# Attention loads: four blocks of values, queries nearer to their use, shorter clears, three loads on ScalarE's queue

## The chip, the cores and the metric

The kernel runs on one core of a Trainium2 chip. The metric is the device time of one execution in microseconds, the median of several runs of the same program. The core has five engines with instruction queues of their own: TensorE (PE in the profile, its weight loads PEld), VectorE (DVE), ScalarE (ACT), GpSimd (POOL) and SyncE (SP). Here SP does nothing but issue transfers between the chip's memory and the core's SBUF; 16 DMA engines carry them out. ScalarE and GpSimd can issue transfers as well.

## The reference, cut to what matters

Three layers follow one another: attention with 8 heads over 4 sequences of 576 tokens (2304 tokens in all), a layer of 8 experts of which each token takes one, and a plain layer with a squared ReLU.

```python
rel = pos[:, None] - pos[None, :]
mask_plain = (rel >= 0) & (rel < 32)                              # heads 0 to 3
mask_dil = (rel >= 0) & (rel < 128) & (rel % 4 == 0)              # heads 4 to 7
attn = softmax(where(mask, q @ k.T / 8, -1e9));  x = attn @ v     # [2304, 512]

e_idx = argmax(x @ w_gate);  gate_w = softmax(x @ w_gate)[e_idx]
eom = sigmoid(x @ w_output_gate)[e_idx]
y[mask] = gate_w * eom * (relu(x[mask] @ w1[e]) @ w2[e])          # mask: e_idx == e

out = (relu(y @ w_in) ** 2) @ w_out
```

## The kernel before, in words

The 2304 tokens are 18 blocks of 128. The attention takes them one after another (the loop over `i` in `attention`); the experts then run over windows of a list of tokens per expert, and the last layer over strips of 768 tokens. The change lies in the attention, with a small part in the ordering of the experts and in the loop for tokens that fit in no window.

**One block of the attention.** `qk_mm` computes the scores of a block with 16 products (32 rows each in the trace), `qk_a` adds the masks on VectorE, `qk_b` takes the maximum on VectorE and subtracts it on GpSimd, `ex` takes the exponential on ScalarE, `tr` transposes the result with the unit matrix on TensorE and copies it out on ScalarE, `pv_mm` multiplies with the values, `pv_x` divides by the sum on VectorE and writes x, and `xt` transposes x for the router. TensorE gets all this in the order in which the loop is written: in iteration `i` it has `tr(i)`, the scores of block `i + 2`, `xt(i - 1)`, and `pv_mm(i)`. So an operand that lands late stops everything behind it on TensorE. Blocks 0 and 1 have their scores ahead of the loop, with warm-up products around them (`warm`).

**The buffers.** Queries lie in three buffers of a pair of blocks (`load_q`). Keys lie in a ring of five blocks (`kf`, `LAP`); after every fifth block `wrap` copies the last block's keys in front of the ring on ScalarE. The values lie in a ring of `VR` blocks (`vb`). Keys and values of two heads stand on alternating partitions with zeros between, so each place of the ring is cleared once by VectorE and GpSimd (`clear_k`, `clear_v`) before its first load.

**The transfers.** Nearly all are issued by SP, in the order in which the program is written. A load waits for the last reader of its buffer, and also for the transfer that was issued eight places earlier, since eight completion semaphores take turns. Where SP waits, all later loads wait with it. Once four blocks or three are done, their x is stored (`store`, five transfers each); the router groups them (`GROUPS`), and each token's entry goes to the list of its expert by an indirect transfer of GpSimd (`scatter`). The lists (`meta_d`, 8 lists of 2560 rows of 64 bytes) are cleared by one transfer (`clear`) at iteration 3. When the first 11 blocks are routed, the largest expert is chosen; SP reads its number and loads its first weights (`load_w`) and the first rows of its list (`meta_load`), at iterations 13 and 14.

**The ordering of the experts.** `order_steps` is a generator: some 50 small VectorE instructions, each set between larger ones of the expert stage (`run_small`). Its last ones compute what the loop over spilled tokens needs (`spilled`), a loop that runs as often as there are groups of tokens beyond all windows.

Of the kernel before, what the change touches and what calls it, by code (L numbers as in the profile page):

```python
# [36 lines left out]
E = 8  # L37
# [5 lines left out]

HALF = WIN[0] // 2
MS = NT + 256
MR = 16
YC = sum(WIN) + 192
NEG = -8.0e9
# [7 lines left out]

VN = 16 * (D + 1)
VL = -(-2 * VN // 128) * 128
VR = 6
KW = (LAP + 1) * 4 * P + 3 * P  # L60


# [9 lines left out]
def attention_experts_kernel(ctx: ExitStack, tc: tile.TileContext, qB, kB, vB, wE, wF, consts, late, rows, out):  # L72
# [30 lines left out]
    er_t = cpool.tile([1, E], I32, name="er_t")  # L103
    of_t = cpool.tile([1, E], I32, name="of_t")
    c0_t = cpool.tile([1, 1], I32, name="c0_t")
    spill = cpool.tile([1, 2, NSPILL], I32, name="spill")
    nspill = cpool.tile([1, 1], I32, name="nspill")
    mt = cpool.tile([P, E + 1, 4, 4], I32, name="mt")

# [4 lines left out]
    def raw_tile():  # L114
        return stg.tile([P, 1024], F32, tag="raw", name="raw", bufs=3)
# [116 lines left out]
    def order_steps(tp):  # L232

        v = nc.vector
        sq, sq2, sp = [1, E, E], [1, 2, E, E], [1, NSPILL, E]

        def row(shape, name, dt=F32):
            return tp.tile([1] + shape, dt, name=name)

        def two(name):  # L240
            return tp.tile([1, E, E], F32, tag="sq", name=name, bufs=2)

        def across(a):
            return a.unsqueeze(1).to_broadcast(sq)

        def down(a):
            return a.unsqueeze(2).to_broadcast(sq)

        cnt = cs[:, 1, :]
        key = row([E], "key")  # L250
        yield v.scalar_tensor_tensor(out=key, in0=cnt, scalar=float(E), in1=rev, op0=ALU.mult, op1=ALU.add)
        yield v.scalar_tensor_tensor(out=key, in0=star[0:1, :], scalar=float(2 ** 20), in1=key, op0=ALU.mult, op1=ALU.add)
        gt = two("gt")
        yield v.tensor_tensor(out=gt, in0=across(key), in1=down(key), op=ALU.is_gt)
        rk = row([E], "rkk")
        yield v.reduce_sum(out=rk, in_=gt, axis=AX.X)
        sel = two("sel")
        yield v.tensor_tensor(out=sel, in0=across(rk), in1=down(io8), op=ALU.is_equal)
        pm = tp.tile([1, NSPILL, E], F32, tag="big", name="pm")[:, 0:2 * E].rearrange("p (a r) e -> p a r e", a=2)
        yield v.tensor_tensor(out=pm, in0=sel.unsqueeze(1).to_broadcast(sq2), in1=cs.unsqueeze(2).to_broadcast(sq2), op=ALU.mult)  # L260
        sr = row([2, E], "sr")
        yield v.reduce_sum(out=sr, in_=pm, axis=AX.X)
        v.tensor_copy(er_t, sr[:, 0, :])
        yield "order"

        def before(a, o):
            om = two("om")
            yield v.tensor_tensor(out=om, in0=across(a), in1=lt, op=ALU.mult)
            yield v.reduce_sum(out=o, in_=om, axis=AX.X)

        nw = row([E], "nw")
        yield v.tensor_tensor(out=nw, in0=sr[:, 1, :], in1=win, op=ALU.min)
        of = row([E], "of")
        yield from before(nw, of)

        big = row([1], "big1")
        yield v.tensor_scalar(out=big, in0=of[:, E - 1:E], scalar1=float(NT - WIN[-1]), scalar2=None, op0=ALU.is_lt)
        yield v.tensor_tensor(out=sr[:, 0, :], in0=win, in1=nw, op=ALU.subtract)
        yield "late"
        yield v.scalar_tensor_tensor(out=nw, in0=sr[:, 0, :], scalar=big, in1=nw, op0=ALU.mult, op1=ALU.add)  # L280
        yield from before(nw, of)
        v.tensor_copy(of_t, of)

        ws = two("ws")
        yield v.tensor_tensor(out=ws, in0=down(rk), in1=across(io8), op=ALU.is_equal)
        yield v.tensor_tensor(out=ws, in0=ws, in1=across(win), op=ALU.mult)
        s0 = row([E], "s0")
        yield v.reduce_sum(out=s0, in_=ws, axis=AX.X)
        yield v.tensor_scalar(out=big, in0=big, scalar1=-1.0, scalar2=1.0, op0=ALU.mult, op1=ALU.add)
        yield v.tensor_scalar(out=s0, in0=s0, scalar1=big, scalar2=None, op0=ALU.mult)  # L290
        yield v.tensor_tensor(out=nw, in0=cnt, in1=s0, op=ALU.subtract)
        yield "offsets"
        ci = row([E], "ci", I32)
        yield v.tensor_scalar(out=ci, in0=nw, scalar1=0.0, scalar2=float(P - 1), op0=ALU.max, op1=ALU.add)
        yield v.tensor_scalar(out=ci, in0=ci, scalar1=7, scalar2=None, op0=ALU.logical_shift_right)
        nt = row([E], "nt")
        yield v.tensor_copy(nt, ci)
        pe = row([E], "pe")
        yield from before(nt, pe)
        yield v.tensor_tensor(out=nt, in0=pe, in1=nt, op=ALU.add)  # L300

        base = row([E], "base")
        yield v.scalar_tensor_tensor(out=base, in0=pe, scalar=-float(P), in1=s0, op0=ALU.mult, op1=ALU.add)
        yield v.tensor_tensor(out=base, in0=base, in1=ems, op=ALU.add)
        ge = tp.tile([1, NSPILL, E], F32, tag="big", name="ge")
        yield v.tensor_tensor(out=ge, in0=io32.unsqueeze(2).to_broadcast(sp), in1=nt.unsqueeze(1).to_broadcast(sp), op=ALU.is_ge)
        ei = row([NSPILL], "ei")
        yield v.reduce_sum(out=ei, in_=ge, axis=AX.X)
        yield v.tensor_scalar(out=ei, in0=ei, scalar1=float(E - 1), scalar2=None, op0=ALU.min)
        yield v.tensor_copy(spill[:, 0, :], ei)  # L310
        yield v.tensor_tensor(out=ge, in0=ei.unsqueeze(2).to_broadcast(sp), in1=io8.unsqueeze(1).to_broadcast(sp), op=ALU.is_equal)
        yield v.tensor_tensor(out=ge, in0=ge, in1=base.unsqueeze(1).to_broadcast(sp), op=ALU.mult)
        yield v.reduce_sum(out=ei, in_=ge, axis=AX.X)
        yield v.scalar_tensor_tensor(out=ei, in0=io32, scalar=float(P), in1=ei, op0=ALU.mult, op1=ALU.add)
        yield v.tensor_scalar(out=ei, in0=ei, scalar1=0.0, scalar2=float(E * MS - P), op0=ALU.max, op1=ALU.min)
        yield v.tensor_copy(spill[:, 1, :], ei)
        yield v.tensor_scalar(out=nt, in0=nt, scalar1=float(NSPILL), scalar2=None, op0=ALU.min)
        yield v.tensor_copy(nspill, nt[:, E - 1:E])
# [24 lines left out]
    def attention():  # L343
# [13 lines left out]
        def warm(n):  # L357

            ps = ps_1.tile([P, 4, P], F32, tag="xt", name="warm")
            for _ in range(n):  # L360
                nc.tensor.matmul(out=ps, lhsT=ones, rhs=ones.unsqueeze(1).to_broadcast([P, 4, P]), start=True, stop=True)

        def load_q(i, n):
            q = wk.tile([P, 2, 4, P], F32, tag="q", name="q", bufs=3)
            a = i % 2
            nc.sync.dma_start(out=q[:, 0:n].rearrange("p i a s -> p (i a s)"), in_=qB[i // 2, :, a:a + n].rearrange("p i s -> p (i s)"))
            for j in range(n):
                q_t[i + j] = q[:, j]

# [22 lines left out]
        def clear_v(j, h2, engine):  # L392
            engine.memset(vb[:, h2, j], 0.0)
# [6 lines left out]
        load_k(1, 1)  # L400
        nc.vector.memset(ones, 1.0)
        warm(8)
        nc.vector.memset(kz[:, :, 0, 0:2, 96:P], 0.0)
        nc.vector.memset(kz[:, :, 0, 2:4], 0.0)
        load_q(1, 1)
        nc.sync.dma_start(out=masks.rearrange("p a b m -> p (a b m)"), in_=consts[:, o:o + 512])
        clear_k(3, nc.vector, nc.gpsimd)
        load_k(2, 1)
        load_q(2, 2)
        nc.sync.dma_start(out=ident, in_=consts[:, 0:P])  # L410
        clear_v(0, 0, nc.vector)
        clear_v(0, 1, nc.gpsimd)
        load_v(0, 1)
# [8 lines left out]
            nc.sync.dma_start(out=late_sb, in_=late)  # L422
            nc.sync.dma_start(out=rowc, in_=rows)

        z = raw_tile().bitcast(I32)[:, 0:MS * E * MR // P // 4]

        def clear():
            nc.sync.dma_start(
                out=meta_d.rearrange("(p a n) c -> p a (n c)", p=P, a=4), in_=z.unsqueeze(1).to_broadcast([P, 4, MS * E * MR // P // 4])
            )  # L430

        group_of = {i: n for n, g in enumerate(GROUPS) for i in g}
        sm_t, p_t, pt_t, o_t, x_t, xT_t, lg_t = {}, {}, {}, {}, {}, {}, {}
# [253 lines left out]
        nc.gpsimd.memset(z.rearrange("p (n c) -> p n c", c=MR)[:, :, 2:3], OOB)  # L687
        nc.gpsimd.memset(idw, 0)
        ex(0)
        load_q(4, 2)  # L690
        load_v(2, 2)
        warm(7)
        ends = {g[-1] + 1: n for n, g in enumerate(GROUPS)}
# [14 lines left out]
        for i in range(NB):  # L708
# [12 lines left out]
                wrap()  # L721
                load_k(n + 2, min(3, NB - n - 2))

            if i % 2 == 0 and i + 6 < NB:
                load_q(i + 6, 2)
            if i == 0:
                load_consts()
            if i == 3:
# [35 lines left out]
                scale(0)  # L764
            if i == NB - 1:
                conv_w(0, 1)
            if i == 0:
                for j in range(4, VR):
                    clear_v(j, 0, nc.vector)
                    clear_v(j, 1, nc.gpsimd)  # L770
                load_v(4, 2)
            if i % 2 == 1 and i + VR - 1 < NB:
                load_v(i + VR - 1, 2)
            if i in STORES:
# [747 lines left out]
    def spilled():  # L1522
# [5 lines left out]
        with ExitStack() as st:  # L1528
            sp = st.enter_context(tc.tile_pool(name="sp", bufs=1))
            ps = st.enter_context(tc.tile_pool(name="sps", bufs=2, space=PSUM))  # L1530
            with tc.For_i(0, total) as i:
                ev = loaded(spill[:, 0, ds(i, 1)], mybir.EngineType.SP, E - 1, "cut to the experts")[0]
                rv = loaded(spill[:, 1, ds(i, 1)], mybir.EngineType.SP, E * MS - P, "cut to the rows")[0]
                m = sp.tile([P, 4], I32, name="m")
                nc.sync.dma_start(out=m, in_=meta_d[ds(rv, P), 0:4])
                x = sp.tile([P, DM], F32, name="sx")
# [147 lines left out]
```

## Time and profile before

| | us |
|---|---|
| median of 3 runs (lowest to highest) | 724.68 (722.94 to 727.16) |
| the profiled execution | 724.47 |
| its span, first to last instruction | 722.8 |

The profile has one execution. Its page says PE 694.7 us busy (96% of the span), DVE 486.4 (67%), ACT 326.5 (45%), POOL 114.5 (16%); the DMA engines moved 138.11 MB at a mean of 191 GB/s, and the granted clock of TensorE was 0.998 of full speed. Times in all rows count from the first instruction. A row of a timeline gives the start, the time taken, the engine, the line, the operation, what it writes and reads, how many instructions were merged into the row, and in brackets how long the engine had been idle and what ended that. SPq is the issuing of a transfer by SP, not the transfer. Since shares over the whole span mix stages, the stretch in which the changed code runs has to be read by itself.

### The profile page before, as it was taken

How to read it: one execution, taken by the hardware profiler on the slowest of the kernel's cores; microseconds unless marked ns; L12 is line 12 of the kernel's file. 1: busy time of each engine (PE TensorE's matmuls, PEld its weight loads, DVE VectorE, ACT ScalarE, POOL GpSimd, SP SyncE). 2: the span in 40 equal slices, each digit the busy share in tenths (PEclk: the TensorE clock that was granted, in tenths of full speed). 3: DMA queues.
4: the chain of work that ended last, by engine and by line, in shares of the span. 5: the costliest groups of instructions: out<-in, count | busy, mean ns of one | idle time of the engine just before them, and what ended most of it. 6: DMA issues, size and time to landing. Idle time of an engine off the chain costs nothing.

```text
span 722.8 us, 13818 instructions
## 1 busy us (share of the span) xinstructions
PE 694.7 (96%) x5203; PEld 631.9 (87%) x5203; DVE 486.4 (67%) x878; ACT 326.5 (45%) x599; POOL 114.5 (16%) x120
## 2 busy tenths in 40 slices
PE   7988889999999999989999999999999999999995
PEld 4766789999999999989999999999988888888884
DVE  7866775773646567668886878787889854445441
ACT  2443544543455555556555545565534422122120
POOL 6245336202010110008000000000000040012003
PEclk9999999999999999999999999999999999999999
DMA  8999556865475776862657545556755453235302
GB/s 281 414 338 316 183 165 210 261 182 162 157 221 158 229 239 190 245 203 64 219 165 249 194 152 195 193 203 231 238 170 196 139 177 108 91 119 162 110 22 91
DMA packets 65503, 138.11 MB, mean 191 GB/s; under 512 B 12838, under 2 KB 40023, under 8 KB 64407
## 3 DMA queue, kind: packets, MB, share of 16 engines
q1 hardware_dynamic: 53538, 121.60, 51.9%
q0 software_dynamic: 3984, 10.22, 4.1%
q10 hardware_dynamic: 7909, 5.35, 2.3%
q8 instruction: 43, 0.70, 0.4%
q14 instruction: 29, 0.24, 0.1%
HBM read 102.06 MB, written 35.12 MB: 190 GB/s over the span
## 4 chain that ended last, share of the span: by engine, by line
PE 68%; issue 10%; DVE 2%; DMA 2%; POOL 1%; ACT 1%; ACTq 0%; POOLq 0%; DVEq 0%; SPq 0%
PE op L1489 6%; PE op L1490 6%; PE op L1491 6%; PE bank_b L881 5%; PE bank_b L879 4%; PE bank_b L880 4%; PE yp L879 4%; PE yp L880 4%; PE hp L879 4%; PE yp L881 4%; PE hp L880 4%; PE hp L881 4%; PE bank_d L881 2%; PE bank_d L880 2%; PE bank_d L879 2%
## 5 line engine op out<-in xcount | busy, mean ns | idle before, releaser
L1454 DVE TENSOR_TENSOR slot_d<-gq,slot_d 128x768 fp32r<-128x768 f32 x48 | 45.9, 957 | 63.8 <-ACT slot_d L1452 62.3
L1452 ACT CAST slot_d<-gq 128x768 fp32r<-128x768 f32 x48 | 40.0, 835 | 95.2 <-PE op L1490 83.1
L1499 POOL DMA_INDIRECT out<-os,idc x18 | 20.0, 1112 | 352.9 <-DVE os L1498 348.3
L893 ACT ACTIVATE hh<-hp 128x240 fp32r<-128x240 f32 (+5 forms) x72 | 29.2, 410 | 42.3 <-PE hp L881 40.4
L1445 DVE SCALAR_TENSOR_TENSOR gq<-gq 128x768 f32<-128x768 f32 x48 | 45.7, 952 | 2.1 <-DMA gq<-g_d 2.1
L173 POOL DMA_INDIRECT xg<-x_d,mt x24 | 25.7, 1069 | 135.2 <-PE xp L197 123.2
L150 DVE TENSOR_TENSOR slot_d<-raw,slot_d 128x1024 fp32r<-128x1024 f32 x24 | 29.2, 1223 | 20.6 <-ACT slot_d L146 20.1
L1489 PE MATMUL op<-slot_b,slot_d 128*128 128x512 f32 x108 | 42.0, 389 | 0.0
L1490 PE MATMUL op<-slot_b,slot_d 128*128 128x512 f32 x108 | 42.0, 389 | 0.0
L1489 PE MATMUL op<-slot_a,slot_d 128*128 128x512 f32 x108 | 42.0, 389 | 0.0
L1490 PE MATMUL op<-slot_a,slot_d 128*128 128x512 f32 x108 | 42.0, 389 | 0.0
L1491 PE MATMUL op<-slot_a,slot_d 128*128 128x512 f32 x108 | 42.0, 389 | 0.0
L1491 PE MATMUL op<-slot_b,slot_d 128*128 128x512 f32 x108 | 42.0, 389 | 0.0
L894 DVE SCALAR_TENSOR_TENSOR hl<-hp,hh 128x240 fp32r<-128x240 f32 (+5 forms) x72 | 31.5, 449 | 14.8 <-ACT hh L893 12.1
L914 ACT COPY ys<-yp 128x240 f32<-128x240 f32 (+5 forms) x36 | 14.4, 399 | 48.8 <-PE yp L881 42.5
L880 PE MATMUL yp<-hl,slot_b 128*128 128x240 f32 (+3 forms) x112 | 31.8, 284 | 0.3 <-DVE hl L894 0.3
L879 PE MATMUL yp<-hh,slot_b 128*128 128x240 f32 (+3 forms) x112 | 32.1, 286 | 0.0
L150 DVE TENSOR_TENSOR slot_b<-raw,slot_b 128x1024 fp32r<-128x1024 f32 x20 | 24.2, 1220 | 11.4 <-ACT slot_b L146 11.0
L881 PE MATMUL yp<-hh,slot_b 128*128 128x240 f32 (+3 forms) x112 | 31.7, 283 | 0.0
L879 PE MATMUL hp<-xh,slot_d 128*128 128x432 f32 (+3 forms) x96 | 30.5, 318 | 0.3 <-DVE hl L894 0.3
L880 PE MATMUL hp<-xl,slot_d 128*128 128x432 f32 (+3 forms) x96 | 30.2, 315 | 0.0
L881 PE MATMUL hp<-xh,slot_d 128*128 128x432 f32 (+3 forms) x96 | 30.2, 314 | 0.0
(338 smaller groups left out, 2277.5 us busy)
## 6 DMA issues: line engine op xcount, KB each, us to landing
raw<-in_wE SPq DMA_DIRECT2D x64, 512.0 KB
g_d<-cr SPq DMA_DIRECT2D x96, 192.0 KB
gq<-g_d SPq DMA_DIRECT2D x48, 384.0 KB
raw<-in_wF SPq DMA_DIRECT2D x32, 512.0 KB
vb<-in_vB SPq DMA_DIRECT2D x16, 520.0 KB
yr<-yT_d SPq DMA_DIRECT2D x16, 384.0 KB
q<-in_qB SPq DMA_DIRECT2D x8, 512.0 KB
kf<-in_kB SPq DMA_DIRECT2D x8, 256.0 KB
```

Source lines behind the costliest of these rows:

```text
L150: nc.vector.tensor_tensor(out=lo, in0=raw_t.pop((r, c)), in1=hi.bitcast(F32), op=ALU.subtract)
L879: nc.tensor.matmul(out=out, lhsT=wh, rhs=mh, start=first, stop=False, skip_group_check=shared)
L880: nc.tensor.matmul(out=out, lhsT=wh, rhs=ml, start=False, stop=False, skip_group_check=shared)
L881: nc.tensor.matmul(out=out, lhsT=wl, rhs=mh, start=False, stop=last, skip_group_check=shared)
L893: nc.scalar.activation(out=h[:, :n], in_=p[:, :n], func=ACTF.Relu)
L894: nc.vector.scalar_tensor_tensor(out=l[:, :n], in0=p[:, :n], scalar=0.0, in1=h[:, :n].bitcast(F32), op0=ALU.max, op1=ALU.subtract)
L1445: nc.vector.scalar_tensor_tensor(out=x, in0=x, scalar=0.0, in1=x, op0=ALU.max, op1=ALU.mult)
L1452: nc.scalar.copy(out=h, in_=x)
L1454: return lambda: nc.vector.tensor_tensor(out=l, in0=x, in1=h.bitcast(F32), op=ALU.subtract)
L1489: nc.tensor.matmul(out=o_t[j], lhsT=h[:, a], rhs=w[:, 0], start=f == 0, stop=False)
L1490: nc.tensor.matmul(out=o_t[j], lhsT=h[:, a], rhs=w[:, 1], start=False, stop=False)
L1491: nc.tensor.matmul(out=o_t[j], lhsT=l[:, a], rhs=w[:, 0], start=False, stop=f == 15)
```

## The change

It has five parts:

1. `VR` falls from 6 to 4. The values of blocks 4 and 5 are no longer loaded into places of their own at iteration 0, whose four clears go; all pairs from block 4 on are loaded at odd iterations into places that have been read, `load_v(i + 3, 2)` instead of `load_v(i + 5, 2)`. The last pair is so issued at iteration 13, behind the first expert weights.
2. Queries: the load of blocks 4 and 5 ahead of the loop goes, and at even iterations `load_q(i + 4, 2)` takes the place of `load_q(i + 6, 2)`.
3. `clear` writes the first 512 rows of each list (`CLEARED`) instead of all 2560. The loop over spilled tokens writes the 128 rows behind a list's end itself; `order_steps` computes those ends (six VectorE instructions more).
4. The masks, the unit matrix and the queries of block 1 are issued by ScalarE instead of SP, behind a small exponential of the ones.
5. The first table load of ScalarE is now that of the small exponential; it is its first instruction in both kernels.

```diff
-VR = 6
+VR = 4
+CLEARED = -(-WIN[0] // 128) * 128
@@ order_steps
+        ends = row([E], "ends")
+        yield v.tensor_tensor(out=ends, in0=cnt, in1=ems, op=ALU.add)
...
+        yield v.tensor_tensor(out=ge, in0=ei.unsqueeze(2).to_broadcast(sp), in1=io8.unsqueeze(1).to_broadcast(sp), op=ALU.is_equal)
+        yield v.tensor_tensor(out=ge, in0=ge, in1=ends.unsqueeze(1).to_broadcast(sp), op=ALU.mult)
+        fi = row([NSPILL], "fi")
+        yield v.reduce_sum(out=fi, in_=ge, axis=AX.X)
+        yield v.tensor_copy(spill[:, 2, :], fi)
@@ attention, ahead of the loop
         warm(8)
+
+        nc.scalar.activation(out=wk.tile([P, 1], F32, tag="first", name="first", bufs=1), in_=ones[:, 0:1], func=ACTF.Exp)
+        nc.scalar.dma_start(out=masks.rearrange("p a b m -> p (a b m)"), in_=consts[:, o:o + 512])
+        nc.scalar.dma_start(out=ident, in_=consts[:, 0:P])
+        load_q(1, 1, nc.scalar)
...
-        load_q(1, 1)
-        nc.sync.dma_start(out=masks.rearrange("p a b m -> p (a b m)"), in_=consts[:, o:o + 512])
...
-        nc.sync.dma_start(out=ident, in_=consts[:, 0:P])
...
-        z = raw_tile().bitcast(I32)[:, 0:MS * E * MR // P // 4]
+        z = raw_tile().bitcast(I32)[:, 0:CLEARED * E * MR // P]
 
         def clear():
-            nc.sync.dma_start(
-                out=meta_d.rearrange("(p a n) c -> p a (n c)", p=P, a=4), in_=z.unsqueeze(1).to_broadcast([P, 4, MS * E * MR // P // 4])
-            )
+
+            d = meta_d.rearrange("(e m) c -> e (m c)", e=E)[:, 0:CLEARED * MR]
+            nc.sync.dma_start(out=d.rearrange("e (p f) -> e p f", p=P // E), in_=z)
...
         ex(0)
-        load_q(4, 2)
         load_v(2, 2)
@@ the loop over blocks
-            if i % 2 == 0 and i + 6 < NB:
-                load_q(i + 6, 2)
+            if i % 2 == 0 and i + 4 < NB:
+                load_q(i + 4, 2)
...
-            if i == 0:
-                for j in range(4, VR):
-                    clear_v(j, 0, nc.vector)
-                    clear_v(j, 1, nc.gpsimd)
-                load_v(4, 2)
             if i % 2 == 1 and i + VR - 1 < NB:
                 load_v(i + VR - 1, 2)
@@ the loop over spilled tokens
+                fv = loaded(spill[:, 2, ds(i, 1)], mybir.EngineType.SP, E * MS - P, "cut to the rows")[0]
+                pad = sp.tile([P, 4], I32, name="pad")
+                nc.vector.memset(pad, 0)
+                nc.vector.memset(pad[:, 2:3], OOB)
+                nc.sync.dma_start(out=meta_d[ds(fv, P), 0:4], in_=pad)
```

What this does to the order of SP's loads at the start shows in SP's list, here before, from the unit matrix to the clear of the lists (q queries, kf keys, vb values, two transfers each for keys and values; a q of 128x1024 is a pair of blocks):

```order
L410 DMA ident<-in_consts 128x128
L383 DMA vb<-in_vB 64x1040 x2
L373 DMA kf<-in_kB 64x1024 x2
L383 DMA vb<-in_vB 64x1040 x2
L366 DMA q<-in_qB 128x1024
L383 DMA vb<-in_vB 64x2080 x2
L373 DMA kf<-in_kB 64x1024 x2
L366 DMA q<-in_qB 128x1024
L422 DMA late_sb<-in_late 128x400
L423 DMA rowc<-in_rows 1x128
L383 DMA vb<-in_vB 64x2080 x4
L373 DMA kf<-in_kB 64x1536 x2
```

The first q of these rows is that of blocks 4 and 5, the second that of blocks 6 and 7. The same place in SP's list with the change:

```order
L391 DMA vb<-in_vB 64x1040 x2
L381 DMA kf<-in_kB 64x1024 x2
L391 DMA vb<-in_vB 64x1040 x2
L391 DMA vb<-in_vB 64x2080 x2
L381 DMA kf<-in_kB 64x1024 x2
L374 DMA q<-in_qB 128x1024
L432 DMA late_sb<-in_late 128x400
L433 DMA rowc<-in_rows 1x128
L391 DMA vb<-in_vB 64x2080 x2
L381 DMA kf<-in_kB 64x1536 x2
L374 DMA q<-in_qB 128x1024
```

Blocks 4 and 5 have moved behind the values of blocks 2 and 3 and the keys of blocks 5 and 6; blocks 6 and 7 behind the keys of blocks 7 to 9; the values of blocks 6 and 7 have left this place.

ScalarE's list begins like this with the change (pr is the exponential of block 0); before, the table load was followed by that exponential at once:

```order
L412 ACT_TABLE_LOAD
L412 ACTIVATE first<-ones 128x1
L413 DMA masks<-in_consts 128x512
L414 DMA ident<-in_consts 128x128
L374 DMA q<-in_qB 128x512
L490 ACTIVATE pr<-sm 128x4x2x64
```

Three transfers stand between the table load and the exponential now, the last of them with a wait for block 0's queries to land.

At the end of the attention SP's list reads as follows with the change (e_t is the number of the chosen expert, raw its weights, mt rows of its list):

```order
L119 TENSOR_LOAD e_t
L142 ISA
L142 DMA raw<-in_wE 128x1024
L168 ISA
L168 DMA mt<-meta_d 128x2x4
L142 ISA
L142 DMA raw<-in_wE 128x1024
L391 DMA vb<-in_vB 64x2080 x2
L142 ISA
L142 DMA raw<-in_wE 128x1024
```

The two vb, the values of blocks 16 and 17, stood before the last keys and ahead of e_t; now they stand behind the second weight.

## Rows read from the trace of the kernel before

**Rows 1.** Busy us of each engine by stretch, with granted clock, DMA share, GB/s

```profile
0.00:88.00 88.00, 74.70 (x1491) 53.68 (x1491) 65.13 (x192) 36.87 (x87) 41.17 (x51) 1.00 0.85 305
...
120.00:400.00 280.00, 276.40 (x1922) 270.08 (x1921) 192.49 (x316) 153.78 (x277) 36.65 (x35) 1.00 0.64 198
```

**Rows 2.** Waits of TensorE from 5 to 90 us: total us, times, longest

```profile
PE s L454 <- issue: 1.9, 5, 0.5
PE o L503 <- issue: 1.9, 2, 1.5
PE lg L563 <- issue: 1.6, 5, 0.4
...
PE s L454 <- DMA kf<-in_kB: 0.4, 1, 0.4
```

**Rows 3.** Busy us by stretch, the first 20 us (DMA share and GB/s last)

```profile
0.00:10.00 10.00, 7.18 (x79) 3.50 (x79) 6.73 (x13) 1.28 (x1) 4.61 (x12) 1.00 0.68 200
10.00:20.00 10.00, 8.05 (x178) 5.92 (x176) 8.74 (x16) 4.34 (x8) 8.00 (x12) 1.00 1.01 384
```

**Rows 4.** Timeline of the first 30 us: start, us, engine, line, operation, idle before

```profile
5.79 1.31 PE L454 MATMUL s<-kf,q 128*32 128x128 f32 x32
...
7.66 1.08 PE L454 MATMUL s<-kf,q 128*32 128x128 f32 x32 [0.56 <-DMA q<-in_qB]
...
8.28 0.69 DVE L468 TENSOR_TENSOR sm<-s,masks 128x512 f32<-128x512 f32 x1 [1.60 <-DMA masks<-in_consts]
...
11.78 0.63 PE L487 MATMUL pt<-ident,pr 128*128 128x128 f32 x4 [1.42 <-DMA ident<-in_consts]
...
19.17 1.08 PE L454 MATMUL s<-kf,q 128*32 128x128 f32 x32
...
20.63 0.63 PE L540 MATMUL xt<-ident,x 128*128 128x128 f32 x4 [0.39 <-DVE x L521]
...
21.42 0.62 ACT L378 COPY kf<-kf 128x512 f32<-128x512 f32 x1
...
26.01 1.08 PE L454 MATMUL s<-kf,q 128*32 128x128 f32 x32
```

**Rows 5.** Timeline of SP's issues

```profile
4.07 0.59 SPq L366 DMA_DIRECT2D q<-in_qB  x1
4.69 0.43 SPq L406 DMA_DIRECT2D masks<-in_consts  x1
...
6.96 0.43 SPq L410 DMA_DIRECT2D ident<-in_consts  x1
...
11.53 0.33 SPq L366 DMA_DIRECT2D q<-in_qB  x1
...
15.77 1.35 SPq L366 DMA_DIRECT2D q<-in_qB  x1
...
19.32 0.48 SPq L383 DMA_DIRECT2D vb<-in_vB  x1
...
22.06 0.81 SPq L373 DMA_DIRECT2D kf<-in_kB  x1
...
23.60 0.58 SPq L366 DMA_DIRECT2D q<-in_qB  x1
```

**Rows 6.** DMA issues, whole span: what, how many, KB each

```profile
vb<-in_vB SPq DMA_DIRECT2D x16, 520.0 KB
...
q<-in_qB SPq DMA_DIRECT2D x8, 512.0 KB
...
meta_d<-raw SPq DMA_DIRECT2D x1, 1280.0 KB
```

**Rows 7.** VectorE by line, 120 to 150 us: busy, mean ns, idle before

```profile
L306 DVE TENSOR_TENSOR ge<-rowc,nt 1x256 f32<-1x256 f32 x1 | 0.4, 402 | 0.0
```

**Rows 8.** Timeline towards the end of the attention, SP and TensorE

```profile
74.97 0.40 SPq L167 DMA_DIRECT2D mt<-meta_d  x1
...
82.91 1.09 PE L503 MATMUL o<-vb,pts 128*32 128x130 f32 x32 [0.69 <-ACT pts L489]
```

More of the change, by code (lines that the diff above doesn't have):

```diff
@@ L105, in attention_experts_kernel @@
     c0_t = cpool.tile([1, 1], I32, name="c0_t")
-    spill = cpool.tile([1, 2, NSPILL], I32, name="spill")
+    spill = cpool.tile([1, 3, NSPILL], I32, name="spill")
     nspill = cpool.tile([1, 1], I32, name="nspill")
@@ L361, in warm, with load_q @@
                 nc.tensor.matmul(out=ps, lhsT=ones, rhs=ones.unsqueeze(1).to_broadcast([P, 4, P]), start=True, stop=True)
-        def load_q(i, n):
+        def load_q(i, n, engine=nc.sync):
             q = wk.tile([P, 2, 4, P], F32, tag="q", name="q", bufs=3)
             a = i % 2
-            nc.sync.dma_start(out=q[:, 0:n].rearrange("p i a s -> p (i a s)"), in_=qB[i // 2, :, a:a + n].rearrange("p i s -> p (i s)"))
+            engine.dma_start(out=q[:, 0:n].rearrange("p i a s -> p (i a s)"), in_=qB[i // 2, :, a:a + n].rearrange("p i s -> p (i s)"))
             for j in range(n):
```

## The prediction

> **What bounds the kernel now.** I read the busy time by stretch first, then TensorE's waits in the first stretch, then that stretch instruction by instruction, then SP's own list of issues beside the DMA rates. From 120 us on TensorE is busy in 276.4 of 280 us, and what comes before 88 us keeps it busy for only 74.7 of 88 [rows 1]. The change works in that first stretch, the attention, and in a few small VectorE instructions behind it. So the question is by how much the end of the attention moves; everything behind hangs on it in a fixed order and, with TensorE full, moves with it one to one.
>
> In the attention TensorE runs in program order, and the waits that name a cause are short: 1.42 us for the unit matrix before the first transposes, 0.56 for the second block's queries, 0.4 for keys [rows 2, 4]. The DMA engines look otherwise: 200 GB/s in the first 10 us at a share of 0.68, then 384 GB/s at a share of 1.01 [rows 3]. From 10 us the transfers are full, and the old order hides that by asking for everything early. That is the point of the whole case: in a full queue the place of a load in the order decides when it lands.
>
> **Start-up.** Block 0's scores end at 5.79 + 1.31 = 7.10 us, and VectorE adds the masks at 8.28, having waited for their landing [rows 4]. The maximum, the subtraction on GpSimd, the exponential and the first transposes at 11.78 follow that addition in a chain. Masks, unit matrix and the second block's queries go to ScalarE's queue, behind its table load and one activation that needs the ones, which VectorE writes among its first instructions; ScalarE has nothing else to do there. SP issued the masks at 4.69 [rows 5]; I estimate two microseconds less. If they land by 7.10, the chain gains 8.28 - 7.10 = 1.2 us, and the wait named for the unit matrix goes with it, since the exponential ends only just before. I take -1.2. Bounds: -1.7 (with the second block's 0.56 gone as well) and +0.5 (if the three loads, now beside SP's, slow the first keys by about that much). Block 4's scores would then start at 17.95 instead of 19.17.
>
> **The queries of blocks 4 and 5.** This is the main term. They were issued at 11.53, ahead of the values of blocks 2 and 3 [rows 5]; now they stand behind those values and behind the keys of blocks 5 and 6. I add the bytes up to and with them in the new order: 6 blocks of queries at 256 KB, 7 of keys at 256, 4 of values at 520 (a pair of blocks is 512 of queries and twice 520 of values [rows 6]), masks 256, unit matrix 64: 5728 KB, or 5.87 MB. The rates deliver 2.00 MB in 10 us and 3.84 MB in the next 10 [rows 3], so the last byte goes at about 20.1 us if the rate is as before. From last byte to released wait I read a lag: the first half of blocks 2 and 3's values ends 4.81 MB into the old order, at 17.3 us, and SP, which allows eight transfers in flight, waits for it until 19.32 [rows 5]: 1.9 us. That gives 22.0 us. SP no longer issues three loads, which took 0.59 + 0.43 + 0.43 = 1.45 us [rows 5], and the DMA engines had room in the first 10 us; I take 0.8 of the 1.45, so 21.2 us, with 20.5 (all of it) and 22.0 (none) as the ends. Block 4's scores, ready at 17.95, wait until 21.2: +3.25.
>
> **What follows block 4.** The clears of value blocks 4 and 5 go: two on VectorE stood before x of block 1, for which TensorE waited 0.39 us at 20.63 [rows 4]. -0.39; bounds -0.4 and 0. The two on GpSimd go with them, and no TensorE wait names them: 0.
>
> Then the queries of blocks 6 and 7. They were issued at 15.77; now they take the place of 23.60 [rows 5], behind the keys of blocks 7 to 9, which need block 4's scores and ScalarE's two wrap copies (the second ends at 21.42 + 0.62 = 22.04 [rows 4], the keys go at 22.06). From block 4 at 21.2: scores end 22.3, 0.8 us for both copies, keys issued 23.1, queries 23.60 - 22.06 = 1.54 us later, 24.6. Block 6's scores stand 26.01 - 19.17 = 6.84 us behind block 4's [rows 4], now 6.45, so at 27.65: a lead of 3.0 us. A load of 256 KB in the light queue of the start took from its issue at 4.07 to 7.66, 3.6 us [rows 4, 5]; 256 KB more at 0.4 MB per us add 0.65. That is 28.9 even without the keys ahead, a wait of 1.2. I take +1.0, since those 3.6 us had a load ahead too; ends 0 (just in time) and +1.6.
>
> The Trainium skill, page "DMA: Bandwidth & Descriptors", section "Anatomy of one DMA — SWDGE (gpsimd) path", gives a fixed cost of about 2.0 us and the bytes at 436 GB/s on top, for loads that GpSimd issues. By that, as an estimate, 512 KB need 3.2 us from issue with nothing ahead, also more than the lead; the wait would be 0.2 us and the sum 726.0. The row says 3.6 us for half the bytes, and the row decides.
>
> TensorE's 0.4 us for keys [rows 2] are those of block 7, at 31.28. It goes, since half of the values that stood ahead of them now come later: -0.4, or 0 if it stays.
>
> **The smaller edits.** The later pairs of queries (blocks 8 to 17) each move behind one load of keys and one of values and keep a lead of about two blocks, 6.8 us: 0, with rival B as the other end. The clear of the lists falls from 1280 KB [rows 6] to 8 lists of 512 rows of 64 bytes, 256 KB. That is 1.05 MB, 2.6 us of the DMA engines, but no TensorE wait behind it is named for the DMA except the 0.4 us counted above: 0, bounds -0.4 and 0. The six additional VectorE instructions of the ordering (one on 8 numbers, four of at most the 256-number kind at 0.40 us [rows 7], one cast) are under 2 us in a stretch where TensorE is full and VectorE works 192.5 of 280 us [rows 1]: 0, up to +0.4 if one of them delays a low part that TensorE wants. What is added to the spill loop runs once per spilled group, and the trace of before holds no instruction of that loop's body: 0.
>
> **Sum.** -1.2 + 3.25 - 0.4 + 1.0 - 0.4 = +2.25 us. The profiled execution took 724.47 us (span 722.8), close to the median of 724.68; 724.5 + 2.3 = 726.8 us. Lowest of the bounds: block 4 at 20.5 instead of 19.17, no wait at block 6: 1.3 - 0.4 - 0.4 = +0.5, or 725.0. Highest: 2.8 + 1.6 = +4.4 with neither gain, or 728.9.
>
> **Rival A: the start carries, faster.** If the loads of blocks 4 to 7 are in time, because the DMA engines run near 384 GB/s from 4 us on with a second queue to fill them, the gains alone stay: -1.2 - 0.4 - 0.4 = -2.0, 722.5 us. For it speaks the share of 0.68 in the first 10 us: room for over 1 MB. Against it: the bytes must be there by 16 us, 4 us ahead of the old delivery, and SP saves 1.45. It goes further if the waits that the trace calls only "issue" (1.9 + 1.9 + 1.6 us [rows 2]) come from the full queue and halve with it: another -2.7, 719.8.
>
> **Rival B: the late blocks starve too.** The values of blocks 16 and 17 now stand in SP's order behind the first two expert weights and the load of the list between them, for which SP waits until 74.97 [rows 8]. They go at about 76, and block 16's product comes at 82.91 [rows 8]: a lead of 6.9 us. Ahead of them and with them are 512 + 1040 KB, 4.0 us at 0.4 MB per us, with 1 us to start and 1.9 of lag: 6.9. It decides as soon as the queue is not empty at 76 us; each microsecond late costs one. (The third weight, now behind them, is only converted after the attention.) The last queries have the same thin lead in a stretch in which the stores of x share the engines. One wait of 1.5 us, or two, on top of the sum: 728.3 to 729.8. Against it: by then 1.05 MB of clears and the early loads no longer fill the queue.
>
> **How the numbers follow.** A measurement of this kernel can tell about 0.5%, 3.6 us: 721.1 to 728.3 us is no change. My forecast, slower by 2.3 us, gets 0.56, and its own range is 725.0 to 728.9; rival A 0.24; rival B 0.20. Of the forecast nine parts in ten lie within 0.5%, of rival B four in five above, of rival A somewhat over a third below. So faster 0.09, same 0.70, slower 0.21. The range reaches from 721.3, which leaves out rival A's far end, to 729.6.
>
> **What would show it.** Right: block 4's scores start at 20.5 to 22 us with a wait for q, block 6's about 7.4 us later, again with a wait for q; the first masks addition comes near 7.1; no wait for keys at block 7; blocks 8 to 13 follow at the old distances. Wrong: block 4's scores before 19 us, or a TensorE that gains on the old distances between blocks 8 and 13 (rival A's second part), or waits for vb at block 16 (rival B).

## The result: slower, and the profile after

The changed kernel takes 730.48 us (median of 7 runs, 725.86 to 732.91) against 723.48 us for the kernel before (7 runs). The ratio is 1.0092, 95% interval 1.0066 to 1.0119: slower by 6.7 us (7.0 by the medians), where +2.3 us was forecast with a range up to 729.6. The profile shows the fastest of the seven executions (725.86 us, span 724.1), so it explains the mechanism but not the whole loss: the first product of the experts starts at 90.86 us in it, only 1.9 us later than before (88.97). The first experiment gives another execution.

TensorE's waits from 5 to 90 us in the changed kernel answer to [rows 2]:

```profile
PE s L464 <- DMA q<-in_qB: 11.2, 7, 4.5
```

11.2 us of waits for queries, seven times, where before there was one of 0.56 us. And the waits called "issue", 5.4 us before, are gone in this execution: TensorE waited for queries instead. Its timeline shows where, as in [rows 4]:

```profile
6.14 1.42 PE L464 MATMUL s<-kf,q 128*32 128x128 f32 x32 [0.29 <-DMA kf<-in_kB]
...
10.93 0.66 PE L497 MATMUL pt<-ident,pr 128*128 128x128 f32 x4 [0.27 <-ACT pr L490]
...
16.85 0.66 PE L497 MATMUL pt<-ident,pr 128*128 128x128 f32 x4
21.98 1.94 PE L464 MATMUL s<-kf,q 128*32 128x128 f32 x32 [4.48 <-DMA q<-in_qB]
23.85 1.12 PE L550 MATMUL xt<-ident,x 128*128 128x128 f32 x4
24.89 1.96 PE L513 MATMUL o<-vb,pts 128*32 128x130 f32 x32
26.79 0.92 PE L497 MATMUL pt<-ident,pr 128*128 128x128 f32 x4
...
31.27 1.08 PE L464 MATMUL s<-kf,q 128*32 128x128 f32 x32 [0.35 <-DMA q<-in_qB]
...
46.33 1.08 PE L464 MATMUL s<-kf,q 128*32 128x128 f32 x32 [0.61 <-DMA q<-in_qB]
...
55.46 1.08 PE L464 MATMUL s<-kf,q 128*32 128x128 f32 x32 [1.13 <-DMA q<-in_qB]
...
64.67 1.08 PE L464 MATMUL s<-kf,q 128*32 128x128 f32 x32 [1.70 <-DMA q<-in_qB]
...
74.08 1.08 PE L464 MATMUL s<-kf,q 128*32 128x128 f32 x32 [2.52 <-DMA q<-in_qB]
...
76.10 1.96 PE L513 MATMUL o<-vb,pts 128*32 128x130 f32 x32
```

Block 4's scores start at 21.98 us instead of 19.17. What the forecast did not have is the column of durations: behind the wait the same products take 1.94, 1.12, 1.96 and 0.92 us, before and elsewhere 1.08, 0.66, 1.09 and 0.66. The windows of that stretch show why (columns as in [rows 1]; the granted clock is the third number from the end):

```profile
20.00:24.00 4.00, 2.02 (x33) 1.53 (x34) 0.00 (x0) 0.00 (x0) 0.00 (x0) 0.57 0.85 331
24.00:28.00 4.00, 4.00 (x53) 3.00 (x57) 2.39 (x5) 0.84 (x3) 1.04 (x1) 0.58 0.63 206
```

TensorE had done nothing from 17.5 to 21.98 us, and then ran at 0.57 and 0.58 of full speed, that is mostly at the lower of its two levels, 1.2 GHz, up to the transposes at 26.79. The same shows once more, shorter, behind the wait of 2.52 us at block 16 (1.96 us at 76.10).

The waits of blocks 10, 12, 14 and 16 follow from SP's issues, against the starts above:

```profile
39.61 0.58 SPq L374 DMA_DIRECT2D q<-in_qB  x1
...
47.37 0.58 SPq L374 DMA_DIRECT2D q<-in_qB  x1
...
58.70 0.36 SPq L374 DMA_DIRECT2D q<-in_qB  x1
...
66.72 0.64 SPq L374 DMA_DIRECT2D q<-in_qB  x1
```

From issue to the start that waited for it: 6.7, 8.1, 6.0 and 7.4 us. The page's list of transfers gives the time from issue to landing as a median, in its last number:

```profile
q<-in_qB SPq DMA_DIRECT2D x8, 512.0 KB, 5.9
```

### The profile page after: what moved, and what is told of

Same layout as the page of the kernel before. It is cut to its first block, busy times and chain, and to the rows that moved or that the text cites. A ratio compares the mean times of both kernels' runs of the same rounds, so it can differ in the third digit from the quotient of the medians.

```text
span 724.1 us, 13819 instructions
## 1 busy us (share of the span) xinstructions
PE 694.0 (96%) x5203; PEld 633.4 (87%) x5203; DVE 486.9 (67%) x881; ACT 327.9 (45%) x600; POOL 113.0 (16%) x118
## 5 line engine op out<-in xcount | busy, mean ns | idle before, releaser
L464 PE MATMUL s<-kf,q 128*32 128x128 f32 x576 | 20.7, 287 | 11.5 <-DMA q<-in_qB 11.2
L883 PE MATMUL hp<-xh,slot_d 128*128 128x432 f32 (+3 forms) x96 | 30.5, 318 | 0.3 <-DVE hl L898 0.3
```

The costliest lines, as they stand in the source:

```text
L883: nc.tensor.matmul(out=out, lhsT=wh, rhs=mh, start=first, stop=False, skip_group_check=shared)
```

## Experiments

Theory T: the queries come too late, everywhere, and TensorE's clock halves behind the longest waits. Its rivals lay the loss on the ring of four blocks of values, on the second queue, or behind the attention. Kernels of one group ran on the same chip; each is compared with the kernel before on that chip (medians 726.84, 726.98, 723.08 and 727.71 us in the four groups), so ratios are compared, not times.

### First group: which part costs

**The change again.**

> The changed kernel once more. Its profile so far is of its fastest execution (725.86 us, six others 729.4 to 732.9). Theory T (queries too late, and TensorE's clock halves behind the long waits): another execution has the same waits for q at blocks 4, 10, 12, 14 and 16 (11 to 16 us in all between 5 and 90 us), and the additional time lies before 120 us, in longer waits for q and further stretches at a granted clock of about 0.5. Theory R (the additional time lies behind the attention, in the added ordering steps or the experts): the stretch before 120 us is as in the profile shown and 120 to 700 us has grown by 4 to 6 us.

733.08 us, ratio 1.0087 (1.0056 to 1.0118). **The queries back:** `load_q(4, 2)` ahead of the loop and `load_q(i + 6, 2)` again; all else of the change stays.

> The changed kernel with the queries loaded as early as before (blocks 4 and 5 ahead of the loop, then i + 6); four blocks of values, short clears and ScalarE's queue stay. Theory T: no wait for q over 0.7 us, no half clock before 700 us, 722 to 724.5 us, equal to before or 1 to 2 us better. Rival V (the value ring of four blocks, or the second queue, is what costs): block 4 in time, but 728 to 731 us all the same.

727.56 us, ratio 1.0006 (0.9974 to 1.0037): no loss, and no gain either. **The queries alone**, in the kernel before:

```diff
-        load_q(4, 2)
...
-            if i % 2 == 0 and i + 6 < NB:
-                load_q(i + 6, 2)
+            if i % 2 == 0 and i + 4 < NB:
+                load_q(i + 4, 2)
```

> The kernel before with the later queries alone; six blocks of values, full clears, all loads on SP. Theory T: a wait for q of 3 to 6 us at block 4 (the values of blocks 4 and 5 do not stand ahead of them, but SP's list is as full as before), half clock behind it, and 728 to 733 us. Rival V: at most 2 us over before, 723 to 726 us.

734.04 us, ratio 1.0090 (1.0064 to 1.0117). Taking the later queries out removes the whole loss, adding them alone makes all of it. Rival V falls; ring, clears and second queue cost nothing that can be told. One part of the expectation for the queries back failed: a stretch at the lower clock is there all the same (granted clock 0.91 from 60 to 80 us, products of 1.96 us at 74.17), behind gaps of 0.3 to 0.7 us.

How one wait becomes 6.8 us is read from the first two of these on the same chip. The change again:

```profile
17.57 0.65 PE L497 MATMUL pt<-ident,pr 128*128 128x128 f32 x4
23.26 1.93 PE L464 MATMUL s<-kf,q 128*32 128x128 f32 x32 [5.03 <-DMA q<-in_qB]
...
28.06 0.89 PE L497 MATMUL pt<-ident,pr 128*128 128x128 f32 x4
```

and with the queries back:

```profile
18.07 0.66 PE L497 MATMUL pt<-ident,pr 128*128 128x128 f32 x4
18.66 1.08 PE L464 MATMUL s<-kf,q 128*32 128x128 f32 x32
...
21.28 0.66 PE L497 MATMUL pt<-ident,pr 128*128 128x128 f32 x4
```

Block 4's scores are 23.26 - 18.66 = 4.6 us later, and up to the next transposes another (28.06 - 23.26) - (21.28 - 18.66) = 2.2 us goes to the slower products: 6.8 us at block 3's transposes. At the first product of the experts the distance is 5.4 us (95.23 - 89.84), at the end the spans differ by 732.4 - 726.1 = 6.3 us. Theory R (behind the attention) is so left with little; and the kernel with the queries back has all the added ordering steps without a loss, the queries alone have none of them and the whole loss. In the change's second execution the waits called "issue" are there:

```profile
PE s L464 <- DMA q<-in_qB: 7.2, 4, 5.0
PE s L464 <- issue: 1.9, 1, 1.9
...
PE lg L573 <- issue: 1.2, 4, 0.4
...
PE o L513 <- issue: 0.6, 2, 0.3
```

3.7 us of them: as much as would make up most of the 4.6 us between the first profile and the median of its runs; that they do is not shown. My count of 11 to 16 us of waits for queries was too high (7.2).

**Warm-up products in the two longest waits.**

```diff
+            if i == 2:
+                warm(16)
+            if i == 14:
+                warm(8)
             if i + 2 < NB:
                 qk(i + 2)
```

> The changed kernel with warm-up products in the two longest waits: 16 ahead of block 4's scores (at 0.24 us each 3.8 of the 4.5 us waited), 8 ahead of block 16's (1.9 of 2.5 us). They compute nothing that is used and shorten no wait. Theory T: the granted clock stays at 1.0 in both places, block 4's scores still start at 21.5 to 22.5 us, and the products behind them take 1.08, 0.66, 1.09 us instead of 1.94, 1.12, 1.96: 2.45 us saved at block 4 and 1.55 at block 16, so 725.5 to 728 us. Rival C (the clock costs nothing that the later slack does not hide): no change, 729 to 732 us.

731.10 us, ratio 1.0066 (1.0039 to 1.0093), 2.0 us under the change on the same chip; the two intervals overlap, so the total alone settles nothing. Theory T's time (725.5 to 728) is missed; 731.10 lies in rival C's. For block 4 the timeline settles it:

```profile
16.68 0.65 PE L497 MATMUL pt<-ident,pr 128*128 128x128 f32 x4
17.18 3.62 PE L369 MATMUL warm<-ones 128*128 128x512 bf16 x16
22.36 1.08 PE L464 MATMUL s<-kf,q 128*32 128x128 f32 x32 [1.57 <-DMA q<-in_qB]
...
24.99 0.66 PE L497 MATMUL pt<-ident,pr 128*128 128x128 f32 x4
```

and its windows:

```profile
20.00:24.00 4.00, 2.43 (x44) 1.45 (x44) 0.42 (x1) 0.00 (x0) 0.00 (x0) 1.00 0.90 352
24.00:28.00 4.00, 4.00 (x105) 3.25 (x104) 3.20 (x7) 2.46 (x6) 1.04 (x1) 1.00 0.79 253
```

From the transposes to the scores it takes 5.68 us, as in the change (5.69): the wait is not shortened. From the scores to the next transposes 2.63 instead of 4.80 us: the lower clock cost 2.2 us, and the engine kept busy, with products that nobody uses, did not lose it. Part of that is lost again at once: block 6 now waits 1.47 us for its queries, 0.23 in the change. At block 16 nothing was saved: in this execution an "issue" wait of 1.86 us came two blocks earlier, and the product behind it ran 1.96 us long.

### Second group: which queries, and which queue

**First pair early:** `load_q(4, 2)` ahead of the loop, later pairs late. **First pair late:** the reverse.

> The changed kernel with the queries of blocks 4 and 5 back ahead of the loop; all later pairs stay late (i + 4). Theory T1 (most of the loss is the first wait with its half clock): block 4 in time, no half clock before 60 us, 0 to 3 us over the kernel before on the same chip. Theory T2 (the later waits of 0.6 to 2.5 us, which grow from block 10 to 16, carry the loss): 4 to 7 us over before.

731.39 us, ratio 1.0053 (1.0031 to 1.0074): between the two theories, over T1's 3 us.

> The changed kernel with only the queries of blocks 4 and 5 late; from iteration 0 on all later pairs are asked for two blocks earlier, as before. T1: block 4's scores wait 4 to 5 us for q, the clock halves for some 7 us, no wait for q from block 8 on, and 4 to 7 us over before. T2: 0 to 3 us over before.

733.38 us, ratio 1.0085 (1.0054 to 1.0117). The first pair alone makes the full loss, as T1 says. But without it over half remains (3.9 us), since the wait and the lower clock move to the next pair, that of block 6:

```profile
25.10 0.66 PE L497 MATMUL pt<-ident,pr 128*128 128x128 f32 x4
29.73 1.08 PE L464 MATMUL s<-kf,q 128*32 128x128 f32 x32 [3.98 <-DMA q<-in_qB]
...
31.79 1.96 PE L513 MATMUL o<-vb,pts 128*32 128x130 f32 x32
```

In the change block 6 waited 0.35 us only: the wait at block 4 had given its queries the time. The waits are not additive: of these two late pairs the one that comes first pays.

**Late queries on ScalarE's queue:** `load_q(i + 4, 2, nc.scalar)`.

> The changed kernel with all its late queries issued by ScalarE instead of SP, in the same iterations. Two views of why they are late: theory S (SP's list: they stand behind transfers for which SP waits, and behind their bytes in one queue): block 4's queries are issued at 12.5 to 13 us instead of 15.8 and land 3 to 4 us later, block 4 waits less than 0.5 us, no half clock, and 0 to 2 us over before. Theory E (the 16 engines are full, whoever asks): 6 us from issue to landing as on SP, so block 4's scores start at 19 to 20 us, later ones wait as in the changed kernel, 3 to 6 us over before. A third way: ScalarE itself waits for one of SP's transfers before it may issue, its exponentials come late, and it is 3 us or more over before with waits for pr and pts.

734.76 us, ratio 1.0100 (1.0069 to 1.0131). Block 4's queries, issued at 11.90, are in time, as theory S has it, but its time of 0 to 2 us over before is missed by far. Now values land late, first at 20 us:

```profile
17.47 1.08 PE L464 MATMUL s<-kf,q 128*32 128x128 f32 x32
...
20.40 1.09 PE L513 MATMUL o<-vb,pts 128*32 128x130 f32 x32 [1.26 <-DMA vb<-in_vB]
```

So the second queue changes who waits. The Trainium skill has the reason (page "DMA: Bandwidth & Descriptors", section "Issuing engines are not separate DMA queues"): transfers started by different engines run on the same 16 DMA engines and interleave there. The trace agrees, with the values' wait of 1.26 us in place of the queries'.

But this wait is not the loss: block 13's transposes start at 66.42 us, 1.55 us behind the kernel with the queries back (64.87). The loss comes behind them, and it comes from SP's list:

```profile
SPq L544 <- DMA q<-in_qB: 7.7, 1, 7.7
```

```profile
71.23 1.88 SPq L391 DMA_DIRECT2D vb<-in_vB  x2
...
78.72 1.96 PE L513 MATMUL o<-vb,pts 128*32 128x130 f32 x32 [2.05 <-DMA vb<-in_vB]
```

In the middle of a store of x SP waits 7.7 us for a transfer of queries that ScalarE had issued. So the values of blocks 14 and 15 go at 71.23 us (63.73 in the change), block 14's product waits 2.05 us for them, and the products behind it run at half clock. At the first product of the experts the kernel is 6.9 us behind the one with the queries back (96.73 against 89.84).

**The start alone:** masks, unit matrix and the second block's queries on ScalarE's queue, in the kernel before.

> The kernel before with one part of the change: masks, unit matrix and the second block's queries on ScalarE's queue. Queries, value ring and clears as before. The forecast's step: the masks land by 7.1 to 7.5 us after the start of block 0's scores instead of 8.3, the first transposes come 0.7 to 1.2 us earlier, and the time is 0.5 to 1.5 us under before, hardly more than can be told. The rival: what the start gains is lost again before 90 us in waits that the trace calls issue (TensorE waiting for its own instructions), and it is within 0.5 us of before.

726.82 us, ratio 0.9998 (0.9979 to 1.0017), with these waits of TensorE from 5 to 95 us first in the list:

```profile
PE o L505 <- issue: 2.3, 3, 1.1
PE s L456 <- issue: 2.1, 4, 0.9
PE lg L565 <- issue: 1.3, 4, 0.6
```

The rival's time holds: of the start's gain nothing can be told at the end. In this execution little of it was there to be lost: block 0's scores took 1.94 us (1.31 before), and the first transposes came at 11.48 us (11.78 before).

### Third and fourth groups: how much lead is enough

**Two pairs early:** blocks 4 to 7 as before, blocks 8 to 17 late.

> The changed kernel with the queries of blocks 4 to 7 as early as before and those of blocks 8 to 17 late (i + 4). Theory L (a lead of two blocks, 6.7 us, is too short for a load that takes 6 to 8 us from issue to landing, wherever it stands; the first late pair takes the wait, since an earlier wait gives the later ones slack): the first long wait for q, 2 to 4 us, moves to block 8 or 10, the clock halves behind it, and it is 3 to 6 us over before. Theory F (only the first 25 us are too full; the waits of the later pairs do not reach the end): 0 to 1.5 us over before.

725.59 us, ratio 1.0034 (1.0010 to 1.0058): 2.5 us over before, between the theories. Blocks 10, 12, 14 and 16 wait 1.07, 0.39, 0.92 and 2.16 us; block 8 does not wait. The loss over before is clear of noise, at half of what I expected; over the kernel with the queries back (1.0006, 0.9974 to 1.0037, on another chip) it is not. It need not be the queries' alone either: behind the 2.16 us, and again behind a wait of 2.18 us before block 16's product, TensorE ran at half clock (products of 1.96 us).

**One block more lead:** blocks 4 and 5 ahead of the loop behind the values, later pairs as `load_q(i + 5, 2)` at odd iterations.

> The changed kernel with every late pair of queries asked for about one block earlier: blocks 4 and 5 ahead of the loop, behind the values of blocks 2 and 3; later pairs at odd iterations as i + 5, ahead of the load of values. Theory L: with a lead of three blocks, some 10 us, against 6 to 8 us from issue to landing, block 4's scores start by 20 us with a wait under 1.5 us, no later wait for q over 0.5 us, no half clock before 60 us: 0 to 2 us over before. Rival (the order at the start is what counts, values and keys ahead of the queries): block 4 still waits 3 us or more and the time is 4 to 7 us over before.

727.93 us, ratio 1.0067 (1.0039 to 1.0096): theory L's time is missed; the time fits its rival's, the wait at block 4 neither's. Block 4 starts at 21.37 us and still waits 2.00: with its queries issued at 14.31 instead of 15.81 us it starts only 0.6 us earlier than in the change. And a new wait stands at block 16:

```profile
75.34 1.09 PE L513 MATMUL o<-vb,pts 128*32 128x130 f32 x32
...
81.91 1.96 PE L513 MATMUL o<-vb,pts 128*32 128x130 f32 x32 [3.50 <-DMA vb<-in_vB]
```

```profile
80.10 0.57 ACT L499 COPY pts<-pt 128x512 f32<-128x512 f32 x1
```

```profile
73.63 0.41 SPq L168 DMA_DIRECT2D mt<-meta_d  x1
74.24 0.35 SPq L142 DMA_DIRECT2D raw<-in_wE  x1
74.69 1.13 SPq L391 DMA_DIRECT2D vb<-in_vB  x2
```

That is the place of rival B of the prediction: the values of blocks 16 and 17 behind the load of the list, 7.2 us from issue to use, then half clock. But not all of the 3.50 us is theirs. The product also reads the copy of the transposed exponential (pts), which ended at 80.67 us; without the values it could have started there, 1.2 us earlier. The rest is ScalarE's, as all of the 0.69 us there in the first profile of the change; it is longer here since ScalarE first waited for a small VectorE instruction of the router, which took 1.82 us instead of 0.19. In the change the same load takes 6.7 us from issue to use in one execution, and the product follows its copy at once (84.14, 84.19); in the other it takes 7.7 us, and the product comes 0.6 us behind its copy (88.30, 88.89).

**The same with those values ahead of the expert weights**, and the **queries back with those values first**; in both the block that begins with `load_w(0, 0)` moves behind `load_v(i + VR - 1, 2)`.

> The kernel of one block more lead, with the values of blocks 16 and 17 ahead of the first expert weights in SP's list, so that they no longer stand behind the load of the list. Theory B (in that kernel 3.5 us of wait for vb at block 16, with a half clock behind it, came from that place): they are issued 4 to 5 us earlier, no wait for vb over 0.5 us, no half clock at 80 to 100 us, and 0 to 2 us over before instead of 4.9. Rival (what is saved there is lost in the weights, which come later): 3 to 6 us over before, with TensorE waiting for the first weights behind 95 us.

733.57 us, ratio 1.0081 (1.0050 to 1.0111). The wait for vb is gone, the time is not. ScalarE, in order, now waits for the first weights ahead of its copy for block 16:

```profile
82.34 1.04 ACT L147 CAST slot_a<-raw 128x1024 fp32r<-128x1024 f32 x1 [1.73 <-DMA raw<-in_wE]
...
83.42 0.57 ACT L499 COPY pts<-pt 128x512 f32<-128x512 f32 x1
```

TensorE waits 1.1 us there. The longer wait comes behind it, since the load of the list is later too: GpSimd gathers the experts' first rows with it, and that stands ahead of its subtraction for block 17.

```profile
83.34 1.06 POOL L174 DMA_INDIRECT xg<-x_d,mt  x1 [4.89 <-DMA raw<-in_wE]
...
85.72 1.05 POOL L485 TENSOR_TENSOR sm<-sm,mx 128x512 f32<-128x512 f32 x1
```

```profile
87.77 1.89 PE L581 MATMUL lg<-late_sb,xT 128*128 128x16 f32 x8 [2.40 <-ACT xT L552]
```

With the queries back that subtraction starts at 81.44 us. Behind the 2.40 us the products are at half clock up to 97 us. The rival's time holds, its place is earlier than it said; block 4 waited 3.47 us here too.

> The changed kernel with its queries as early as before and the values of blocks 16 and 17 ahead of the first expert weights: the parts of the change that cost nothing, with both late loads mended. A hope for a version that beats both: 1 to 3 us under before. The sober view: the start's gain of about 1 us does not reach the end, as with the start alone, and it is within 0.5% of before, -1 to +1 us.

728.90 us, ratio 1.0019 (0.9998 to 1.0040): the sober view. Its profile, of one of the slowest executions (732.4), has the same late gather and a wait of 2.63 us with half clock behind it, so the late loads are not mended but exchanged. No version here beats the kernel before by more than the noise.

## Why the prediction was wrong, point by point

- **The queries of blocks 4 and 5**, the main term: place, cause and sign were right. The landing was at the end of my bounds in one execution (21.98 us; 21.2 taken, 22.0 with nothing saved by SP) and beyond them in the next (23.26), so the wait itself was too short: 3.25 us against 4.48 and 5.03. The step that failed is its price, "wait until 21.2: +3.25": I took a wait as its own length. Behind it TensorE ran at half its clock for 5.7 us, another 2.2 us, which stood nowhere in the sum. No row of before shows this in the attention (granted clock 1.00 to 88 us, [rows 1]); its longest wait there was 1.5 us [rows 2]. The Trainium skill has it (page "TensorE: Matmul & The Clock Gate", section "Part 1: The HAM clock gate (the "warmup" mystery)"): the clock goes to 1.2 GHz where the engine idles. The trace agrees, with 0.58; the forecast had not weighed it.
- **Start, -1.2, keys and clears, -0.4 each:** seen in part in the trace, not in the time. In the first profile the first transposes come at 10.93 instead of 11.78 us, 0.85 earlier (block 0's scores begin 0.35 later, waiting for keys, as the upper bound of that step had it), in the second execution at 11.65; block 7 no longer waits. But the start alone, and the whole change with its queries back, are at 0.9998 and 1.0006. Of the 2.0 us of gains that I counted nothing can be told at the end; the intervals reach down to -1.5 and -1.9 us.
- **Block 6, +1.0:** 0.35 us, and its scores came 9.3 us behind block 4's, where I had 7.4. The two query terms together, 3.25 + 1.0, are close to the 4.6 us measured at block 4, but by luck: one was too small, the other too large.
- **So the sum closes**, if none of the gains arrive: +2.25, plus those 2.0, plus 2.2 of clock is +6.5; measured +7.0 and, on another chip, +6.2 (medians).
- **The later pairs, 0:** I gave them a lead of 6.8 us and called it enough; from issue to use they need 6 to 8. They wait 0.6 to 2.5 us in the change, and the kernel with the first two pairs early is 2.5 us over before. Behind the wait at block 4 they add nothing that can be told (ratio 1.0085 with the first pair late alone, 1.0087 with all).
- **Rival A** (the waits called "issue" shrink): to nothing in one execution, to 3.7 of 5.4 us in the next. It made the profile look harmless, not the kernel fast. **Rival B:** the place is real where the attention is less late (one block more lead), with 1.2 us of waiting that is the values' own.
- The Trainium skill's fixed cost and rate for loads by GpSimd (page "DMA: Bandwidth & Descriptors", section "Anatomy of one DMA — SWDGE (gpsimd) path") would give, as an estimate, 3.2 us for 512 KB. These loads, issued by SP and with others ahead of them, took 5.9 us in the median; the measurement decides.

What stays open: why the "issue" waits are 0 in one execution and 2 to 6.5 us in others, which waits the lower clock follows, and by which of the loads' places the 6 to 8 us from issue to use could be shortened; asking 1.5 us earlier gave 0.6. Each kernel was profiled in one execution, the change in two.

## What to carry to other kernels

In a full transfer queue the lead of a load is compared with its time from issue to landing as measured under that load (here 5.9 us in the median, 6 to 8 us up to the start that waited, for 512 KB), never with that in a light queue. A wait of TensorE is priced with what its clock does afterwards: read the granted clock and the durations of the next products, not the gap alone. And before an early gain is counted, look whether it is still there when the stage ends.

## What the runs showed of the hardware

- One wait can cost half as much again: the 4.48 us of the change, the 3.98 of the kernel with the first pair early and the 3.50 with one block more lead were each followed by products at half clock (1.94 to 1.96 us instead of 1.08 or 1.09), 2.2 us more where it was measured. 3.6 us of unused products in the same gap kept the clock at 1.00.
- The length of a wait alone does not tell: behind 2.00 us (one block more lead, block 4) the next products took their 1.08 and 1.09 us, behind 2.16 us (two pairs early, block 16) the product with the values took 1.96. And with the queries back a product of 1.96 us stands behind four gaps of 0.30 to 0.71 us, where the kernel before, behind four gaps of 0.32 to 0.71 us, shows 1.09.
- The spread of one and the same kernel goes with that clock: over 23 runs of the kernel before on one chip the fastest, 719.12 us, had a mean granted clock of 0.998, the slowest, 728.00 us, one of 0.988 (correlation over the 23 runs -0.82; -0.51 to -0.58 in the three other groups). That is a correlation, not a cause shown.
- Waits of TensorE for its own instructions ("issue") can be absent from an execution of a kernel and present in the next: none with 11.2 us of waits for queries in the first profile of the change, 3.7 us with 7.2 in the second. They do not simply take the queries' place: the queries alone show 6.5 us of them beside 7.1 us for queries.
